# A piece of weight conversion four steps earlier in attention, and what follows it in the load queue

## The chip, the cores and the metric

The kernel runs on one core of a Trainium2 chip. The metric is the device time of one execution in microseconds. Engines: PE (matmul, with PEld for its weight loads), DVE (vector), ACT (scalar), POOL (GpSimd), and SP (SyncE), which issues nearly all DMAs here from one queue in program order.

## The reference

Three layers in fp32, one behind the other:

- attention with capped scores over 4 x 12 heads, 448 positions, 64 wide: `s = cap * tanh(q k^T / 8 / cap)`, softmax over the keys, times v. The result is read as x, 1792 tokens of 768.
- a soft mixture of 8 experts with 4 slots each: `logits = x @ phi`; a softmax over the tokens gives each slot its input `d^T x`; every expert computes `relu(slot @ w1[e]) @ w2[e]` (w1 768 x 1024, w2 1024 x 768); a softmax over the slots gives `c`, and the layer returns `c @ slot_out`.
- an MLP with a learnt slope: `h = x @ w_in`, `g = max(h, 0) + alpha * min(h, 0)`, `g @ w_out` (w_in 768 x 2048, w_out 2048 x 768).

`w_in`, `w_out` and `alpha` of the MLP come to the chip as the reference draws them; w_in and w_out arrive as 64-bit numbers (pairs of 32-bit words), which the kernel turns into fp32 itself.

## The kernel before, in words

**Attention** (lines 227 to 755) works on 24 pairs of heads. A pair has four steps, one for each chunk of keys, in the order CHUNKS = 0, 3, 1, 2 (chunk 3 is the short tail of the keys of both heads). Step `g` (line 702) issues `qk` of pair `g // 4` (scores on PE, then Tanh and Exp on ACT into a tile `p` of the pool `pt`), in the second step of a pair also the transposes of the next pair's k and q (`trans_k`, `trans_q`, with DVE and ACT passes for the high and low parts), then background work that was put off with `later` (row sums `rs`, norms `rb`, natural x `nx`, logits `lg`, `lr`, slot sums `ss`), then loads and conversions, and last `pv` of two steps before (matmuls `o`; POOL adds the rows of p into `acc`, lines 396, 400, 403). So p has its readers two steps after it is written. The program is handed to a scheduler that orders each engine's instructions; every engine then runs its own list in order.

**Conversion of w_in.** w_in is cut in 24 pieces of 128 x 512. A buffer `cvbuf` (line 652), which is one of the eleven 12 KB weight slots (number NA - 1 = 10), holds two raw pieces and two converted halves. `cv_at(n)` (line 663) names the step of piece n: 4, 6, 9, 13, 17, 21, ... and 93 for piece 23, the second step of pair 23. `conv_w_in` (line 667) is one ACT pass and four DVE passes (`to_f32`, lines 178 to 190). Two steps later `store_w_in` (line 673) writes the piece to a scratch tensor in HBM and loads the raw piece n + 2. After the last store the slot joins the free list.

**Weight loads.** `loads` (lines 81 to 89) is the order in which weights are fetched: w1 and w2 of the experts in halves of 12 KB per partition, then w_in and w_out. In attention `load_next` (line 121) may run in the fourth step of the pairs in LOADS (line 55), if a slot is free: ten of the eleven slots are filled at pairs 2 to 20, the entry 22 finds none free, and the entry 23 fills slot 10 behind the last store. `load_early` (line 116) fetches QE = 1 quarter (3 KB per partition) of the twelfth load in pair 21, into a tile of its own.

**Tail** (lines 757 to 1033). Behind attention's pools, which end there, a pool `xtra` takes their memory for seven more slots in quarters of 3 KB (line 1018): 27 loads (line 111, the twelfth load's first quarter is there already). Each of them waits for the attention tiles that it lies on. Then `experts` (line 800) runs expert by expert: h (line 810), ReLU, transposes, y (line 832). `done_with` frees a slot when its weight has been used, and `load_free` issues the next load into it, on SP's queue behind all earlier ones. After expert 7, `gather` and `mlp` (line 862): the first layer (`a_block`, line 870, and `hidden`), and the second (lines 941 to 948) with w_out split in high and low parts (`split_wo`).

**Attention's pools** lie behind the weight slots in the order of lines 232 to 246: nat0, nat1 (q and k as loaded, 4,096 bytes each), stk0 (transposed, 7,680), vn0 (1,792), acc0 (3,584), stk1 (7,680), pt (four buffers, 14,336 with the padding of the short chunk's), vn1, acc1, aconst0 (sel, hot, phi: 4,096), xn (7 x 1,792), xu (4 x 2,048), xnat (2 x 2,048), sm, aconst. Even pairs use the pools with 0, odd ones those with 1. The xtra quarters lie over them in steps of 3,072 bytes, quarter 0 at nat0's start.

Of the kernel before, what the change touches and what calls it, by code (L numbers as in the profile page):

```python
# [8 lines left out]
F32 = mybir.dt.float32  # L9
# [15 lines left out]
def tile_attention_soft_moe_mlp(ctx, tc, q, k, v, cap, phi, w1, w2, w_in, w_out, alpha, out):  # L25
    nc = tc.nc
    B, H, S, D = q.shape
    J = 4
# [4 lines left out]
    NSLOT = phi.shape[1]  # L33
# [12 lines left out]
    JK = 3  # L46
# [5 lines left out]
    LAG = 2  # L52

    CHUNKS = (0, 3, 1, 2)
    LOADS = (2, 4, 6, 8, 10, 12, 14, 16, 18, 20, 22, 23)

    EH = 5
    TBS = (4, 2, 2, 2, 2, 2)
# [38 lines left out]
    def may_load():  # L97
        if nload[0] == len(loads):
            return None
        late = loads[nload[0]][0] in ("wi", "wo")  # L100
        fit = [n for n in free if not late or n < NA]
        return fit[0] if len(fit) > (late and kept[0] < NWO) else None
# [124 lines left out]
    def attention():  # L227
        with ExitStack() as pools:
            def pool(name, bufs=1, **kw):
                return pools.enter_context(tc.tile_pool(name=name, bufs=bufs, **kw))  # L230
# [4 lines left out]
            v_0 = pool("vn0")  # L235
            acc_0 = pool("acc0")
            stk_1 = pool("stk1")
            pt_p = pool("pt", 4)
            v_1 = pool("vn1")
            acc_1 = pool("acc1")  # L240
            ac0_p = pool("aconst0")
# [3 lines left out]
            sm_p = pool("sm")  # L245
# [12 lines left out]
            phi_rep = ac_p.tile([128, 128], F32, name="phi_rep")  # L258
            z_run = ac_p.tile([128, 1], F32, name="z_run")

            def head(u):
                return slice(64 * u, 64 * u + 64)
# [6 lines left out]
            nat, stk, sc_t, pt, acc, ov, xu, xn = {}, {}, {}, {}, {}, {}, {}, {}  # L269
# [7 lines left out]
            def matmul(*a, **kw):  # L277
                ins = nc.tensor.matmul(*a, **kw)  # L278
                if order:
                    if order[0] is not None:  # L280
                        tc.add_manual_dep(ins.ins, order[0].ins.name, NOSYNC, reason="tilings together")
                    order[0] = ins
                return ins
# [81 lines left out]
            def qk(i, c):  # L365

                kh, kl = stk["k", i]
                qh, ql = stk["q", i]
                ps = ps_s.tile([128, 2, 512], F32, tag="s", name="s")
                for n, (a, b) in enumerate(((kh, qh), (kh, ql), (kl, qh))):  # L370
                    flags = dict(start=(n == 0), stop=(n == 2))
                    if c == JK:
                        matmul(ps[:, 0, :S], a[:, KEYS:], b, **flags)
                        continue
                    for u in range(2):
                        o = 128 * c
                        matmul(ps[:, u, :S], a[head(u), o:o + 128], b[head(u)], **flags)
                n = 1 if c == JK else 2
                pe = pt_p.tile([128, n, S], F32, tag="p", name="p")
                nc.scalar.activation(out=pe, in_=ps[:, :n, :S], func=AF.Tanh)  # L380
                nc.scalar.activation(out=pe, in_=pe, func=AF.Exp, scale=cap_sb)  # L381
                pt[i, c] = pe
# [277 lines left out]

            ncv = KD * (DFF // 512)

            def cv_at(n):

                return J + 2 * n if n < 2 else J * n + 1

            def conv_w_in(i):
                fb, kk = divmod(i, KD)
                t = cvbuf[:, 2, i % 2 * 512:i % 2 * 512 + 512].bitcast(F32)
                to_f32(craw.pop(i), t, (order[0], latest[0]))  # L670
                cout[i] = t
# [30 lines left out]
            for g in range(NPAIR * J + LAG):  # L702
                now[0] = g
                i, c = divmod(g, J)
# [4 lines left out]
                if i < NPAIR:  # L709
                    qk(i, CHUNKS[c])  # L710
                    if c == 1 and i + 1 < NPAIR:
                        trans_k(i + 1)
                        trans_q(i + 1)
                run_bg()
                if i < NPAIR:
                    if c == 0:
                        last = load(i + 2, "kq") or last
                    if c == 2:
                        if i == NPAIR - LAG - 1:
                            load_early(last)  # L720
                    if g == 2:
                        load_w_in(0)
                        load_w_in(1)
                    for n in range(ncv):
                        if cv_at(n) == g - 2:
                            store_w_in(n)
                        if cv_at(n) == g:
                            conv_w_in(n)
                    if c == 3 and i in LOADS and may_load() is not None:
                        load_next(last)  # L730
                if g >= LAG:
                    n, e = divmod(g - LAG, J)
# [7 lines left out]

            nc.vector.tensor_scalar(out=z_run, in0=z_run, scalar1=1e-9, scalar2=None, op0=ALU.add)
            nc.vector.reciprocal(out=z_run, in_=z_run)
            diag = sm_p.tile([128, NSLOT], F32, tag="diag", name="diag")
            nc.vector.tensor_scalar(
                out=diag, in0=stackI[:, 0:NSLOT], scalar1=z_run, scalar2=None, op0=ALU.mult
            )
# [10 lines left out]
    def tail():  # L757
# [254 lines left out]
        with (  # L1012
# [3 lines left out]
            with tc.tile_pool(name="ex2", bufs=1, reuse_waits="tile", side="right") as ex2_p:  # L1016
# [6 lines left out]
                with (  # L1023
# [9 lines left out]
                    mlp(ps_w, ps_c, ex_p, cv_p, g_p, ob_p, so, cstk)  # L1033

    attention()
    tail()

# [29 lines left out]
```

## Time and profile before

| | us |
|---|---|
| median of 3 runs | 623.11 (621.99 to 629.77) |
| the profiled execution | 622.67 |
| its span, first to last instruction | 620.7 |
| PE busy | 578.6 (93%) |
| DVE busy | 394.7 (64%) |
| ACT busy | 319.3 (51%) |
| POOL busy | 160.1 (26%) |
| DMA from HBM to the chip and back | 98.41 MB read, 11.80 MB written |

Attention ends at about 274 us, the experts at about 349, and the rest is the MLP. A busy share is an average over these three stages. Times in the rows are counted from the span's start. PE's matmuls are pipelined, so a row of x8 may overlap its neighbours by some tenths of a microsecond. "[2.65 <-DMA w<-...]" behind a row is the idle time of that engine before it and what ended it.

### The profile page before, as it was taken

What the parts mean: (1) busy time and instruction counts of PE and PEld (TensorE: products, weight loads), DVE (VectorE), ACT (ScalarE), POOL (GpSimd) and SP (SyncE); (2) the same over time, 40 slices, a digit from 0 to 9 for tenths busy, and PEclk for the clock granted to TensorE, in tenths of its full rate; (3) what the DMA queues carried; (4) which work ended last, traced back from release to release, by engine and by line L of the source; (5) the groups of instructions that cost most, each with busy time, mean ns of one, the idle gap of its engine ahead of it and who ended that gap; (6) DMA issues with size and microseconds to landing.
All of it is one profiled execution on the core that took longest, in us unless ns stands there. A gap on an engine that the chain in (4) does not pass through costs nothing.

```text
span 620.7 us, 10735 instructions
## 1 busy us (share of the span) xinstructions
PE 578.6 (93%) x4110; PEld 384.7 (62%) x4110; DVE 394.7 (64%) x734; ACT 319.3 (51%) x509; POOL 160.1 (26%) x111
## 2 busy tenths in 40 slices
PE   6799898999999999989896899999999999999996
PEld 4344344455445445454452568888888888888886
DVE  4568667696769879640013399999566666666662
ACT  4798898888889687420101266764412121121211
POOL 0668668475848457100000000000000000000000
PEclk9899999999999999979998899999999999999999
DMA  4786897887978661599999999200301001010101
GB/s 103 199 260 158 260 265 214 261 213 210 262 227 265 207 171 53 194 373 370 403 404 407 389 402 408 102 1 1 103 1 51 1 21 32 0 52 2 51 1 51
DMA packets 95169, 110.90 MB, mean 179 GB/s; under 512 B 56208, under 2 KB 70032, under 8 KB 95120
## 3 DMA queue, kind: packets, MB, share of 16 engines
q1 hardware_dynamic: 94976, 110.24, 55.0%
q8 instruction: 32, 0.52, 0.3%
q14 instruction: 17, 0.14, 0.1%
q10 hardware_dynamic: 144, 0.00, 0.0%
HBM read 98.41 MB, written 11.80 MB: 178 GB/s over the span
## 4 chain that ended last, share of the span: by engine, by line
PE 64%; DMA 15%; DVE 8%; ACT 7%; POOL 3%; issue 1%; SPq 1%; ACTq 0%; POOLq 0%
PE oc L941 13%; PE oc L947 13%; PE oc L948 13%; DMA w<-in_moe_w_dram 12%; PE o L278 6%; PE s L278 5%; ACT p L381 2%; PE hps L896 2%; PE aps L870 2%; ACT p L380 2%; DMA q<-in_q_dram 2%; POOL acc L400 2%; PE rs L278 1%; DMA cvbuf<-in_moe_w_in_dram 1%; PE nx L278 1%
## 5 line engine op out<-in xcount | busy, mean ns | idle before, releaser
L947 PE MATMUL oc<-wsp,gh 128*128 128x512 f32 x448 | 151.7, 339 | 0.0
L941 PE MATMUL oc<-wsp,gh 128*128 128x512 f32 x448 | 151.6, 338 | 0.0
L948 PE MATMUL oc<-wsp,gl 128*128 128x512 f32 x448 | 150.7, 337 | 0.0
L912 ACT ACTIVATE gh<-gf 128x256 fp32r<-128x256 f32 (+1 forms) x96 | 43.5, 453 | 133.0 <-DVE gf L911 127.1
L278 PE MATMUL o<-p,v 128*64 128x448 f32 (+1 forms) x384 | 94.0, 568 | 10.1 <-ACT xu L405 10.0
L380 ACT ACTIVATE p<-s 128x896 f32<-128x896 f32 x96 | 79.0, 824 | 28.6 <-PE s L278 19.7
L381 ACT ACTIVATE p<-p,cap 128x896 f32<-128x896 f32 x96 | 91.2, 951 | 2.3
L941 PEld LDWEIGHTS oc<-wsp,gh 128*128 128x128 f32 x448 | 85.0, 190 | 10.7 <-issue 0.9
L948 PEld LDWEIGHTS oc<-wsp,gl 128*128 128x128 f32 x448 | 84.7, 189 | 11.1 <-issue 1.2
L947 PEld LDWEIGHTS oc<-wsp,gh 128*128 128x128 f32 x448 | 85.0, 190 | 9.7 <-issue 0.4
L913 DVE TENSOR_TENSOR gl<-gf,gh 128x256 fp32r<-128x256 f32 (+1 forms) x96 | 45.0, 469 | 45.3 <-ACT gh L912 45.2
L396 POOL TENSOR_TENSOR acc<-p 128x896 f32<-128x896 f32 x24 | 53.0, 2207 | 77.8 <-ACT p L381 77.8
L278 PEld LDWEIGHTS s<-qh,kh 64*128 64x128 f32 (+1 forms) x168 | 18.1, 186 | 67.1 <-ACT p L380 26.1
L400 POOL TENSOR_TENSOR acc<-acc,p 64x448 f32<-64x448 f32 x46 | 54.3, 1180 | 3.1
L908 DVE TENSOR_SCALAR mn<-hps,alpha 128x256 f32<-128x256 f32 (+1 forms) x81 | 39.5, 487 | 23.6 <-PE hps L896 23.5
L403 POOL TENSOR_TENSOR acc<-acc,p 128x896 f32<-128x896 f32 x23 | 49.0, 2129 | 1.8
L278 PE MATMUL s<-qh,kh 64*128 64x448 f32 (+1 forms) x168 | 45.8, 475 | 0.0
L278 PEld LDWEIGHTS o<-p,v 128*64 128x64 f32 (+1 forms) x384 | 19.0, 134 | 34.8 <-ACT xu L405 16.4
L911 DVE SCALAR_TENSOR_TENSOR gf<-hps,mn 128x256 f32<-128x256 f32 (+1 forms) x81 | 34.6, 427 | 2.7
L278 PE MATMUL s<-qh,kl 64*128 64x448 f32 (+1 forms) x168 | 35.5, 367 | 0.0
L278 PE MATMUL s<-ql,kh 64*128 64x448 f32 (+1 forms) x168 | 35.3, 365 | 0.0
L810 PE MATMUL h<-w,slotT 128*32 128x256 f32 x384 | 30.6, 418 | 4.5 <-DMA w<-in_moe_w_dram 4.5
(151 smaller groups left out, 771.6 us busy)
## 6 DMA issues: line engine op xcount, KB each, us to landing
w<-in_moe_w_dram SPq DMA_DIRECT2D x80, 384.0 KB, 8.4
w<-in_moe_w_dram SPq DMA_DIRECT2D x36, 512.0 KB, 8.2
cvbuf<-in_moe_w_in_dram SPq DMA_DIRECT2D x24, 512.0 KB, 4.5
w<-in_moe_w_out_dram SPq DMA_DIRECT2D x16, 768.0 KB, 8.9
w_in<-cvbuf SPq DMA_DIRECT2D x24, 256.0 KB, 2.4
q<-in_q_dram SPq DMA_DIRECT2D x48, 112.0 KB, 4.0
k<-in_k_dram SPq DMA_DIRECT2D x48, 96.0 KB, 5.1
v<-in_v_dram SPq DMA_DIRECT2D x24, 192.0 KB, 3.4
```

What stands on the lines that cost most here:

```text
L278: ins = nc.tensor.matmul(*a, **kw)
L380: nc.scalar.activation(out=pe, in_=ps[:, :n, :S], func=AF.Tanh)
L381: nc.scalar.activation(out=pe, in_=pe, func=AF.Exp, scale=cap_sb)
L396: nc.gpsimd.tensor_add(out=a, in0=pt[i, 0], in1=pe)
L400: nc.gpsimd.tensor_add(out=a[r, u, :], in0=a[r, u, :], in1=pt[i, JK][r, 0, :])
L403: nc.gpsimd.tensor_add(out=a, in0=a, in1=pe)
L908: nc.vector.tensor_scalar(out=mn, in0=ps, scalar1=0.0, scalar2=alpha_sb[:, f:f + 1], op0=ALU.min, op1=ALU.mult)
L912: nc.scalar.activation(out=gh, in_=gf, func=AF.Copy)
L913: nc.vector.tensor_sub(out=gl, in0=gf, in1=gh)
L941: ins = nc.tensor.matmul(o, gh[:, ts], wo_h[f][:, cols], start=(f == 0 and not second), stop=False)
L947: nc.tensor.matmul(o, gh[:, ts], wo_l[f][:, cols], start=False, stop=False)
L948: nc.tensor.matmul(o, gl[:, ts], wo_h[f][:, cols], start=False, stop=(f == KF - 1 and not more))
```

## The change

The steps of the pieces come from a list: 4, 7, 10, 13, 16, 19, 22, 25, 29, and from there every fourth step, so that piece 23 is converted in step 89, the second of pair 22, and stored in step 91. LOADS has 21 and 22 for its last two entries. The pool `pt` has three buffers, and the short chunk's p has a pool of its own with one buffer of 1,792 bytes. `diag` takes the first columns of `phi_rep` and needs no tile.

```diff
-    LOADS = (2, 4, 6, 8, 10, 12, 14, 16, 18, 20, 22, 23)
+    LOADS = (2, 4, 6, 8, 10, 12, 14, 16, 18, 20, 21, 22)
...
-            pt_p = pool("pt", 4)
+            pt_p = pool("pt", 3)
+            ptt_p = pool("ptt")
...
-                pe = pt_p.tile([128, n, S], F32, tag="p", name="p")
+                pe = (ptt_p if c == JK else pt_p).tile([128, n, S], F32, tag="p", name="p")
...
+            cv_steps = [4, 7, 10, 13, 16, 19, 22, 25, 29]
+            while len(cv_steps) < ncv:
+                cv_steps.append(cv_steps[-1] + J)
+
             def cv_at(n):
-
-                return J + 2 * n if n < 2 else J * n + 1
+                return cv_steps[n]
...
-            diag = sm_p.tile([128, NSLOT], F32, tag="diag", name="diag")
+            diag = phi_rep[:, :NSLOT]
```

## Rows read from the trace of the kernel before

**Rows 1.** Windows, 360 to 370 us: PE, PEld, DVE, ACT, POOL busy, clock, DMA share, GB/s.

```profile
360.00:370.00 10.00, 10.00 (x57) 5.67 (x56) 9.68 (x16) 6.31 (x12) 0.00 (x0) 1.00 1.03 409
```

**Rows 2.** The chain of waits in order of time, 225 to 360 us: start, length, what.

```profile
340.73 7.88 DMA w<-in_moe_w_dram
348.65 0.63 PE y L832 x6
```

**Rows 3.** Windows around and after attention's end, columns as in rows 1.

```profile
246.40:254.50 8.10, 7.96 (x63) 3.40 (x63) 5.34 (x10) 6.85 (x9) 4.27 (x3) 1.00 0.10 34
...
264.00:284.00 20.00, 16.98 (x195) 10.60 (x197) 6.47 (x21) 3.00 (x8) 0.59 (x2) 0.83 1.07 371
284.00:324.00 40.00, 36.47 (x524) 19.94 (x520) 3.91 (x15) 3.51 (x13) 1.59 (x6) 1.00 1.04 395
324.00:350.00 26.00, 18.96 (x184) 7.06 (x177) 6.04 (x10) 2.50 (x4) 0.31 (x1) 0.87 1.04 399
```

**Rows 4.** DMA share in tenths, 40 slices of the span (15.5 us each).

```profile
DMA  4786897887978661599999999200301001010101
```

**Rows 5.** Timeline of SP's queue, 215 to 350 us: start, length, line, tiles, count.

```profile
244.32 6.93 SPq L675 DMA_DIRECT2D w_in<-cvbuf  x2
254.54 1.76 SPq L157 DMA_DIRECT2D w<-in_moe_w_dram  x4
256.34 28.26 SPq L111 DMA_DIRECT2D w<-in_moe_w_dram  x27
```

**Rows 6.** Issue to landing: the two stores of 244 to 251, then the 27 quarters.

```profile
DMA to landing us min/median/max: 2.0/2.7/3.5
...
DMA to landing us min/median/max: 6.5/8.6/9.4
```

**Rows 7.** Timeline of PE, the last two experts.

```profile
322.22 2.94 PE L810 MATMUL h<-w,slotT 128*32 128x256 f32 x47
...
328.33 2.51 PE L832 MATMUL y<-w,hT 128*32 128x256 f32 x30
...
334.45 0.64 PE L810 MATMUL h<-w,slotT 128*32 128x256 f32 x8 [2.65 <-DMA w<-in_moe_w_dram]
```

**Rows 8.** Timeline of PE, attention's end and expert 0.

```profile
253.37 0.55 PE L278 MATMUL rs<-acc,hot 128*32 128x224 f32 x6
...
256.64 1.07 PE L278 MATMUL rs<-p,hot 128*32 128x224 f32 x16
...
269.69 1.06 PE L278 MATMUL ss<-xu,dl 112*32 112x128 f32 x32
...
274.16 4.51 PE L810 MATMUL h<-w,slotT 128*32 128x256 f32 x48
```

**Rows 9.** The tile cvbuf: ns min/median/max of a pass; ACT's idle time before one.

```profile
L178 ACT ACTIVATE cvbuf<-cvbuf x24: 657/672/686, 21.7 to 247.1; 128x512 f32<-128x512 f32 x24
L179 DVE TENSOR_SCALAR cvbuf<-cvbuf x24: 408/417/1522, 22.3 to 247.9; 128x512 f32<-128x512 f32 x24
L183 DVE TENSOR_SCALAR cvbuf<-cvbuf x24: 417/427/2214, 23.9 to 249.0; 128x512 uint32<-128x512 uint32 x24
L186 DVE SCALAR_TENSOR_TENSOR cvbuf<-cvbuf x24: 681/693/1520, 24.8 to 249.5; 128x512 uint32<-128x512 uint32 x24
L189 DVE SCALAR_TENSOR_TENSOR cvbuf<-cvbuf x24: 680/692/2573, 26.0 to 250.2; 128x512 uint32<-128x512 uint32 x24
...
  DMA cvbuf<-in_moe_w_in_dram: 1.7, 1
```

**Rows 10.** Windows, pairs 3 to 5, columns as in rows 1.

```profile
43.00:62.50 19.50, 17.43 (x114) 8.05 (x110) 17.07 (x23) 17.39 (x24) 14.32 (x9) 1.00 0.75 190
```

**Rows 11.** Timelines of DVE and POOL at piece 22's last pass.

```profile
241.83 2.47 DVE L189 SCALAR_TENSOR_TENSOR cvbuf<-cvbuf 128x512 uint32<-128x512 uint32 x1
...
240.82 2.92 POOL L396 TENSOR_TENSOR acc<-p 128x896 f32<-128x896 f32 x1 [3.06 <-ACT p L381]
```

## The prediction, made before the changed kernel was run

> **What bounds the kernel now.** I read the profile from its end backwards. The last stage, the MLP, has no slack: PE is busy 10.00 of 10 us at full clock [rows 1], so whatever moves its start moves the end by as much. Before it the chain of waits is one unbroken run of weight transfers up to 348.61 us, and the last six matmuls of the last expert (y) start 0.04 us after the last one [rows 2]. So the expert stage ends with a DMA stream. The windows show that stream: from 264 us on, the 16 DMA engines are full (share 1.04 to 1.07, 371 to 399 GB/s), but from 246.40 to 254.50 they are almost idle (0.10, 34 GB/s) [rows 3]. The row of slices says the same: a 1 in the sixteenth slice (232.8 to 248.3 us), a 5 behind it, then nines [rows 4]. The stream is therefore late because it starts late.
>
> Why it starts late is on SyncE's queue [rows 5]. In attention's last pairs SyncE does little but wait: the store of w_in piece 22 goes at 244.32, that of piece 23 at 250.92 (244.32 + 6.93 - 0.33), and only behind that, at 254.54, come the four quarters for the slot that was the conversion buffer, and at 256.34 the 27 quarters that lie on attention's own memory. The gap from 250.92 to 254.54 is the last store landing (3.5 us, the longer of the two [rows 6]).
>
> The expert stage is not DMA-bound all along. PE works without a wait on DMA through the next-to-last expert (h from 322.22, y to about 331.2), and waits in the last: 2.65 us before its first h, then 0.2 to 0.6 us before almost every group [rows 7]. Seven experts were on chip or ahead; the eighth is late.
>
> **The change part by part.**
>
> *Last piece four steps earlier.* Pieces from the ninth on (index 8) move up one place: index 8 goes at step 29, where index 7 went, and index 23 at step 89, where index 22 went. Pair 23 has no conversion. So the store that now goes at 244.32 becomes the last one. It lands 2.0 us later (the shorter of the two [rows 6]; 3.5 is the other bound), and the slot's four quarters follow at about 254.54 - 250.92 - 3.5 = 0.1 us behind the landing: 244.32 + 2.0 + 0.1 = 246.4, against 254.54. The stream starts 8.1 us earlier (6.6 with a landing of 3.5). The step's queue order allows it: the store frees the slot and the load stands right behind it in the same step (LOADS has 22); the last v load on SyncE is two steps before. LOADS' 21 finds no free slot and does nothing.
>
> *Do the next quarters follow?* They wait in order for attention's buffers. By the shapes in the code, quarters 0 to 4 lie on q and k of pairs 22 and 23 as loaded and on pair 22's transposed ones, all read by step 91, the step of the store at 244.32; 5 and 6 on the sums of pair 22, read by rs until 253.92; 10 to 14 on pair 23's p and acc, read until 257.71; 15 to 19 on sel, phi and xn, read before ss starts at 269.69; 20 to 24 on xu and xnat, which ss reads until 270.75 [rows 8]. The 27 issues took 28.26 us, 1.05 each [rows 5], so quarter k would now be due at 248.2 + 1.05 k: the fifth at 253.5, the tenth at 258.7, the twentieth at 269.2 (with the pools behind pt 1,792 bytes lower it is number 20, no longer 21, that first touches xu), the load behind them at 276.6. That last one needs the slots of expert 0's h, which ends at 274.16 + 4.51 = 278.67 [rows 8]. So issues wait 0.4, 0, 1.6 and 2.1 us (number 15, due at 264.0, 5.7 at the very most), each below the 8.6 us that a transfer spends in flight behind others [rows 6]: the engines don't run dry, and the stream keeps its lead.
>
> *What the lead is worth.* 8.1 us if each transfer takes as long as before; if the extra stretch runs at the 371 GB/s of 264 to 284 and saves time at 399 [rows 3], 8.1 x 371/399 = 7.5. I take 7.9, nearer to the first, because a lead of the whole queue carries each transfer's own length with it. Its cover on the other side: the last y ends at 348.65 + 0.63 = 349.3, so 341.4 then; PE alone, from 331.2 with the 9.0 us of the expert before it (322.22 to 331.2), would reach 340.2 [rows 7]. So DMA still ends last, by about 1 us, and more than 9.1 us can't be had here.
>
> The Trainium skill, DMA: Bandwidth & Descriptors (Where 436 GB/s comes from), says that HBM to SBUF is held to about 358 GB/s for a core. The trace disagrees: 395 and 399 GB/s over 66 us [rows 3]. By that rule the lead would give 8.1 x 358/399 = 7.3.
>
> *First nine three steps apart.* Steps 6, 9, 17, 21 and 93 become 7, 10, 16, 19 and 22. The work is the same: each conversion has one ACT pass of 0.672 us and four DVE passes of 0.417 + 0.427 + 0.693 + 0.692 = 2.23 us [rows 9]. One more of them falls into the first 25 steps, one fewer into the last pair. Load (512 KB) and store of a piece move with it; the pieces get four steps or more from load to conversion, as most have now; the one wait of ACT on such a landing in the whole run, 1.7 us [rows 9], is the first piece's, and that stays at step 4. In two of the cases (steps 11 and 19) store and load of w_in no longer stand just before a slot's load, and the q and k behind them can only gain. DVE from 43.0 to 62.5 is busy 17.07 of 19.50 and ACT 17.39 [rows 10]; one more conversion takes DVE to 19.3, just inside. If the passes of ACT at steps 9, 17 and 21 come off the path the gain is 3 x 0.672 = 2.0 us, if all five new places cost theirs the loss is 3.4; I take 0 and keep both.
>
> *Pools and diag.* pt held four buffers in a cycle of four, chunk by chunk the same; three and a separate one give every chunk the same distance to its former reader: 0. Both bounds are 0 because no wait changes. diag in phi_rep's place overwrites a tile whose last reader, the last logits matmul, stands before the softmax that diag waits for anyway: 0. The 1,920 bytes freed are under the 3,072 that one more early quarter takes, and the diff leaves QE at 1: I find no extra early quarter. With one, 1.0 us more would be saved (393,216 bytes at 395 GB/s).
>
> **Sum.** The profiled execution took 622.67 us (span 620.7 and 2.0 around it): 622.67 - 7.9 = 614.8. The median of the runs shown is 0.44 above that execution, so I forecast 615.
>
> **The rivals.**
>
> *The queue starves behind attention's buffers.* Only the slot's four quarters come early, then SyncE stands until the old time because a later quarter waits for more than I read from the shapes. For it: SyncE is in order, and a quarter touches up to three tiles. Against: 5 is the first one with a late reader. Four quarters at 1.0 us each: 4.0 saved, 618.7.
>
> *Attention gets longer (slower).* The moved conversions fall beside POOL's adds. The row shows what that does: the last pass of piece 22 took 2.47 us instead of 0.69 while POOL's add ran from 240.82 to 243.74 [rows 11], and the four maxima add to 1.522 + 2.214 + 1.520 + 2.573 = 7.83 against 2.23, 5.6 more [rows 9]. Five of them lose 28.0 at most; DVE's slack of 2.43 in 19.5 us [rows 10] gives 5.4 over the 16 steps concerned (98 steps end at about 266 us, 2.7 each: 43 us); 22.6 remain, less 7.9: 14.7 slower, 637. The sign turns where the five lose 13.3 together, 2.7 each. Against: the maxima are single passes, and the medians say that most passes meet no add.
> The Trainium skill, SBUF — State Buffer (SBUF: two separate sides), says why: VectorE passes in a two-port mode or with two SBUF inputs and GpSimd's share one pair of ports, and the one that starts second waits for the whole of the other. By that rule every moved conversion can meet it; the 2.47 us pass, ending 0.56 after the add's end, agrees.
>
> *Attention gets shorter as well.* The 2.0 us of ACT above come off and q lands earlier: 612.8 or a little under. For it: the queue is shorter at steps 11 and 19. Against: POOL and PE are nearly full too.
>
> *It doesn't do what it says.* The slot is not free in pair 22 and loads at the old time: 622.7. Against: the store appends the slot before the load asks.
>
> **How the numbers follow.** Forecast (613 to 617) 0.60; starved queue 0.17; shorter attention 0.10; no effect 0.05; slower 0.08. The range takes in the starved queue, the gain of 2.0 with an extra quarter, and the loss of 3.4 with a landing of 3.5: 611 to 621, about 0.83. 2% is 12.5 us, about what a measurement of this kernel can tell from no change: faster needs under 610.7, beyond what PE leaves in the expert stage, 0.05; slower needs over 635.6, the disturbed conversions nearly at their maximum, 0.03; within 2%: 0.92.
>
> **What would show it.** After the change: SyncE's row of the slot's quarters at about 246.4; DMA share near 1 from 248 us on; h of expert 0 still at 274; the last y at about 341, its waits on DMA shorter; MLP unchanged in length. Wrong if the share falls below 0.9 for more than 2 us between 250 and 285, if expert 0 starts later than 276, or if the last expert waits for PE's own work and the end moves by less.

## The result: 0.9% faster, with a last store 8 us earlier within attention and an attention that is 4 us longer

| | before | after |
|---|---|---|
| median of 20 runs each | 624.25 us | 618.36 us |
| ratio, 95% interval | | 0.9909 [0.9885, 0.9934], about -5.7 us |
| profiled execution, its span | 622.67, 620.7 | 618.59, 616.2 |
| last score tile of attention (step 95) starts | 252.33 | 256.12 |
| last store of w_in issued, landed | 250.93, 254.38 | 248.12, 250.12 |
| the slot's quarters issued | 254.54 | 250.26 |
| last y of the expert stage ends | 349.29 | 345.01 |

The forecast was 615; the median came 3.4 us above it, outside the narrow range of 613 to 617 and inside the wide one of 611 to 621. Each ratio here and below is taken against runs of before made beside that kernel's (median 624.25 here, 622.86 to 623.42 for the experiments), and two single runs far above the rest (712.54 us of e5, 798.61 of before) are left out of it. The table says where the 3.4 went. In the profiled execution the slot's quarters left 4.3 us earlier and not 8.1, because the end of attention runs 3.8 us late. First SP's queue after the change (start, length, line, tiles, count), which answers to [rows 5]:

```profile
248.12 0.33 SPq L680 DMA_DIRECT2D w_in<-cvbuf  x1
250.26 1.76 SPq L157 DMA_DIRECT2D w<-in_moe_w_dram  x4
252.07 29.08 SPq L111 DMA_DIRECT2D w<-in_moe_w_dram  x27
```

The store lands 2.0 us later, the quarters follow 0.14 behind, and the 27 go at 1.08 us each (forecast 1.05): as forecast, only 3.9 us later than forecast. (In the changed kernel the lines of the helpers are one higher and those behind the conversions five.) ScalarE's row of the last score tile, before and then after, has the same 3.8:

```profile
252.33 0.92 ACT L380 ACTIVATE p<-s 128x896 f32<-128x896 f32 x1
```

```profile
256.12 0.92 ACT L381 ACTIVATE p<-s 128x896 f32<-128x896 f32 x1
```

The windows of after (columns as in rows 1), to set beside [rows 1, 3], and its slices of DMA share beside [rows 4]:

```profile
246.40:250.30 3.90, 3.56 (x30) 1.82 (x27) 3.27 (x5) 2.94 (x5) 3.76 (x3) 1.00 0.18 67
250.30:264.00 13.70, 13.46 (x107) 5.69 (x107) 7.34 (x13) 7.30 (x10) 4.21 (x2) 1.00 0.93 318
264.00:284.00 20.00, 17.18 (x144) 10.96 (x144) 8.05 (x24) 3.71 (x9) 0.00 (x0) 0.74 1.07 370
284.00:324.00 40.00, 36.25 (x508) 21.18 (x511) 3.48 (x15) 3.68 (x14) 1.56 (x5) 1.00 1.03 401
324.00:345.00 21.00, 18.78 (x249) 9.52 (x248) 6.16 (x10) 2.41 (x4) 0.62 (x2) 1.00 1.03 399
355.50:365.50 10.00, 10.00 (x56) 5.63 (x55) 9.68 (x16) 6.31 (x12) 0.00 (x0) 1.00 1.02 408
```

```profile
DMA  4778877798887781799999999100301010010101
```

From 250 us on the stream is nearly full (share 0.93 up to 264, 1.02 or more behind it), and the MLP has no slack, as before. In the row of slices the trough is one slice (1, then 7) instead of a 1 and a 5. PE's timeline (answers to [rows 7, 8]) shows the changed end of the expert stage:

```profile
273.98 1.93 PE L279 MATMUL ss<-xu,dl 112*32 112x128 f32 x32
...
279.42 4.29 PE L815 MATMUL h<-w,slotT 128*32 128x256 f32 x48
...
335.74 2.94 PE L815 MATMUL h<-w,slotT 128*32 128x256 f32 x47
...
343.38 0.63 PE L837 MATMUL y<-w,hT 128*32 128x256 f32 x6 [0.36 <-DMA w<-in_moe_w_dram]
344.38 0.63 PE L837 MATMUL y<-w,hT 128*32 128x256 f32 x6 [0.37 <-DMA w<-in_moe_w_dram]
```

The last expert's h no longer waits for DMA (2.65 us before its first group in [rows 7]); only the last groups of y do, by 0.4. PE and the stream now end within a microsecond of each other.

**The account of the profiled execution.** Between the start of step 95's tile and the slot's quarters lay +2.21 us, now -5.86: the place of the last piece brings 8.07 (the store 6.60 earlier, its landing 2.00 instead of 3.45). Attention gives back 3.79. From the slot's quarters to the last y it is 94.75 us in both. The rest of the span is 0.18 shorter, what lies around the span 0.38 longer. -8.07 + 3.79 - 0.18 + 0.38 = -4.08, the difference of 618.59 and 622.67. The medians differ by 5.9, since this execution of before lies 1.6 below its median and that of after 0.2 above its own; the ratio gives 5.7.

### The profile page after: what moved, and what is told of

Its sections match the earlier page's. It is cut to its first block, busy times and chain, and to the rows that moved or that the text cites. A ratio compares the mean times of both kernels' runs of the same rounds, so it can differ in the third digit from the quotient of the medians.

```text
span 616.2 us, 10737 instructions
## 1 busy us (share of the span) xinstructions
PE 574.9 (93%) x4110; PEld 386.6 (63%) x4110; DVE 403.6 (65%) x734; ACT 318.8 (52%) x509; POOL 162.4 (26%) x111
## 4 chain that ended last, share of the span: by engine, by line
PE 64%; DVE 11%; DMA 10%; ACT 7%; POOL 4%; issue 2%; SPq 1%; ACTq 0%; POOLq 0%
PE oc L946 13%; PE oc L952 13%; PE oc L953 13%; DMA w<-in_moe_w_dram 7%; PE o L279 5%; PE s L279 5%; PE hps L901 2%; ACT p L382 2%; POOL acc L401 2%; PE aps L875 2%; POOL acc L397 2%; ACT p L381 2%; DMA k<-in_k_dram 2%; PE h L815 2%; PE tr L279 1%
## 5 line engine op out<-in xcount | busy, mean ns | idle before, releaser
L837 PE MATMUL y<-w,hT 128*32 128x256 f32 x384 | 30.7, 382 | 1.8 <-DVE hT L830 1.1
```

## Why attention is longer, read from the two traces

Four microseconds do not come at once. Against before, the score tile of step 13 starts 0.7 later, that of step 21 0.6, of step 22 2.8, of step 37 4.05, and from step 42 on every tile is 3.8 late. The largest step, 2.2 us, is that from 21 to 22, behind the second conversion of pair 4. The other 1.6 (0.6 up to step 21 and 1.0 from step 22 to 42) was not traced. GpSimd's timeline of before in this stretch (in brackets the idle time ahead):

```profile
55.41 2.35 POOL L396 TENSOR_TENSOR acc<-p 128x896 f32<-128x896 f32 x1 [2.35 <-ACT p L381]
57.83 2.67 POOL L400 TENSOR_TENSOR acc<-acc,p 64x448 f32<-64x448 f32 x2
60.57 2.11 POOL L403 TENSOR_TENSOR acc<-acc,p 128x896 f32<-128x896 f32 x1
65.07 2.10 POOL L396 TENSOR_TENSOR acc<-p 128x896 f32<-128x896 f32 x1 [2.39 <-ACT p L381]
```

Per pair GpSimd adds without a break for 7 us and has one gap, of 2.4 us. The conversion in VectorE's timeline of before stands exactly in the gap from 62.68 to 65.07:

```profile
62.79 0.42 DVE L179 TENSOR_SCALAR cvbuf<-cvbuf 128x512 f32<-128x512 f32 x1
63.25 0.43 DVE L183 TENSOR_SCALAR cvbuf<-cvbuf 128x512 uint32<-128x512 uint32 x1
63.71 0.69 DVE L186 SCALAR_TENSOR_TENSOR cvbuf<-cvbuf 128x512 uint32<-128x512 uint32 x1
64.43 0.69 DVE L189 SCALAR_TENSOR_TENSOR cvbuf<-cvbuf 128x512 uint32<-128x512 uint32 x1
```

62.79 to 65.12: 2.33 us in a gap of 2.39. The second conversion of pair 4 after the change has no gap. GpSimd, then VectorE, of after:

```profile
56.05 2.45 POOL L397 TENSOR_TENSOR acc<-p 128x896 f32<-128x896 f32 x1 [2.27 <-ACT p L382]
58.57 2.50 POOL L401 TENSOR_TENSOR acc<-acc,p 64x448 f32<-64x448 f32 x2
61.15 2.43 POOL L404 TENSOR_TENSOR acc<-acc,p 128x896 f32<-128x896 f32 x1
67.83 2.11 POOL L397 TENSOR_TENSOR acc<-p 128x896 f32<-128x896 f32 x1 [4.26 <-ACT p L382]
```

```profile
57.99 0.79 DVE L179 TENSOR_SCALAR cvbuf<-cvbuf 128x512 f32<-128x512 f32 x1
58.81 1.25 DVE L183 TENSOR_SCALAR cvbuf<-cvbuf 128x512 uint32<-128x512 uint32 x1
60.09 1.52 DVE L186 SCALAR_TENSOR_TENSOR cvbuf<-cvbuf 128x512 uint32<-128x512 uint32 x1
61.65 2.48 DVE L189 SCALAR_TENSOR_TENSOR cvbuf<-cvbuf 128x512 uint32<-128x512 uint32 x1
64.05 0.61 DVE L487 TENSOR_TENSOR xn<-xu,rb 128x448 f32<-128x448 f32 x1
```

Each pass ends just behind one add (0.3 to 0.55 us): one pass per add, 6.14 us instead of 2.33 (57.99 to 64.13). Attention's own xn stands behind them on VectorE, xu on ScalarE waits 2.06 for xn, and o on PE 2.25 for xu:

```profile
64.75 0.55 ACT L406 ACTIVATE xu<-o 128x448 f32<-128x448 f32 x1 [2.06 <-DVE xn L487]
```

```profile
65.35 0.97 PE L279 MATMUL o<-p,v 128*64 128x448 f32 x4 [2.25 <-ACT xu L406]
```

ScalarE's next score tile, that of step 22, stands behind xu and starts at 65.76. GpSimd's next pair then starts late: 4.26 idle instead of 2.39. The Trainium skill, SBUF — State Buffer (SBUF: two separate sides), agrees: an operation of VectorE in a two-port mode or with two SBUF inputs and one of GpSimd exclude each other for a whole instruction.

## The experiments

What each run's profile shows, one execution each, in us from its span's start ("second conversion" names the step of the one that shares a pair with another, beyond those of before):

| kernel | last conversion | second conversion | tile of step 95, against before | slot's quarters | last y ends | quarters to last y |
|---|---|---|---|---|---|---|
| before | 93 | | 0 | 254.54 | 349.29 | 94.75 |
| before again | 93 | | +1.3 | 255.73 | 350.12 | 94.4 |
| after | 89 | 19 | +3.8 | 250.26 | 345.01 | 94.75 |
| e1, steps alone | 89 | 19 | +4.2 | 250.70 | 345.00 | 94.3 |
| e2 | 93 | 19 | +4.1 | 256.81 | 351.61 | 94.8 |
| e3 | 89 | 58 | +9.3 | 255.83 | 349.94 | 94.1 |
| e4, fewer passes | 89 | 19 | -0.2 | 246.27 | 340.91 | 94.6 |
| e5 | 91 | 91 | +8.7 | 255.63 | 350.48 | 94.9 |
| e6 | 89 | 83 | +4.1 | 248.46 | 344.24 | 95.8 |
| e7 | 89 | 11 | +4.8 | 251.29 | 345.80 | 94.5 |
| e9 | 89 | 19 | +2.3 | 248.75 | 343.60 | 94.9 |
| e10 | 93 | | +1.2 | 255.72 | 350.79 | 95.1 |
| e11 | 92 | | +3.9 | 258.17 | 352.47 | 94.3 |
| e12, fewer passes | 89 | 19 | +7.6 | 254.15 | 349.09 | 94.9 |

Two things can be read at once. The last column moves by 1.7 at most (94.1 to 95.8) while the start moves by 12: nearly all that the stream's start gains or loses reaches the end of the expert stage. And the start is attention's length plus the place of the last piece.

**Which part of the change does it.** The kernel before with the new list of steps alone:

```diff
-                return J + 2 * n if n < 2 else J * n + 1
+                return cv_steps[n]   # [4, 7, 10, 13, 16, 19, 22, 25, 29, 33, ...]
```

> The kernel before with the new list of conversion steps alone; pools, diag and LOADS as before. If the steps are the whole change: a span of 616.2 us within 0.5, the slot's quarters issued at 250.3, score tiles of step 95 about 3.8 us later than before. If the pools, diag or LOADS have a part: a span nearer to 620.7 or a different shift in attention.

618.32 us (one run); attention 4.2 longer, last y at 345.00. The first expectation came out: the steps are the whole change, and the pools, diag and the list of load steps move nothing that can be seen in one execution.

**The two effects apart.** The new early places, the last piece back at 93:

```diff
+            cv_steps[-1] = 93
-    LOADS = (2, 4, 6, 8, 10, 12, 14, 16, 18, 20, 21, 22)
+    LOADS = (2, 4, 6, 8, 10, 12, 14, 16, 18, 20, 22, 23)
```

> The changed kernel with the first nine pieces three steps apart, but the last piece back in step 93 (LOADS 22, 23). If the three-step spacing costs attention 3.8 us by itself: step 95 about 3.8 us later than before, the slot's quarters at about 254.5 + 3.8 = 258.3, and an end 3 to 4 us later than before, 626 to 627 (ratio about 1.006). If the attention is longer for another reason, such as the last piece's place or the pools: as before, 622.7.

625.06 us, ratio 1.0024 [0.9996, 1.0052]. Attention is 4.1 longer; the last store goes 3.4 later, but lands after 2.3 us instead of 3.45, so that the quarters leave 2.3 later and not 3.8. So the early places by themselves bring nothing; that they cost something is seen in the profile, while by the times no change is not excluded. Against this kernel, after differs in the place of the last piece (and the two load steps) alone: its quarters leave 6.55 earlier, its last y ends 6.60 earlier, and its ratio is 0.9909 instead of 1.0024. This is the lead, without a change of the early places.

**The vector passes taken out.** In the kernel after, pieces 1, 2, 4, 5 and 6 keep only ScalarE's pass:

```diff
-                to_f32(craw.pop(i), t, (order[0], latest[0]))
+                if i in (1, 2, 4, 5, 6):
+                    ins = nc.scalar.activation(
+                        out=t, in_=craw.pop(i)[..., 1].bitcast(F32), func=AF.Abs, scale=65536.0
+                    )
+                    tc.add_manual_dep(ins.ins, order[0].ins.name, NOSYNC, reason="not before its step")
+                else:
+                    to_f32(craw.pop(i), t, (order[0], latest[0]))
```

> The changed kernel without the four vector passes of the five moved pieces (1, 2, 4, 5, 6): their scalar pass, their store and their loads stay, and what is stored for them is the scalar pass's result. If the vector passes beside POOL's adds are what lengthens attention: the shift of +3.8 us at step 40 goes to 0 or below (down to -2), the end to 614.5 or less. If the scalar pass in another place or the order of SyncE's queue is the cause: the shift stays at 3 to 4 us and the end at 617 to 618.

613.91 us (one run, 3.0 below the fastest of 20 of after). SP's queue, and PE's last y:

```profile
244.12 0.33 SPq L686 DMA_DIRECT2D w_in<-cvbuf  x1
246.27 1.76 SPq L157 DMA_DIRECT2D w<-in_moe_w_dram  x4
```

```profile
340.27 0.63 PE L843 MATMUL y<-w,hT 128*32 128x256 f32 x6 [0.35 <-DMA w<-in_moe_w_dram]
```

The forecast had 244.32, 246.4 and 341.4 for these three. With the passes gone everything else of the prediction comes out: attention is as long as before's (0.2 shorter), and the stream's term is confirmed. So what attention pays for is in the passes. The run takes out twenty of them, though, and doesn't only put them elsewhere.

**Another place for the one conversion more.** The twenty-four conversions stood in 23 pairs, one in each and two in the first of them. If the last pair has none, another must have two. Old early places, the extra one in pair 14:

```diff
+            cv_steps = [4, 6, *range(9, 54, J), 56, 58, *range(61, 90, J)]
```

> The changed kernel with the pieces at their old steps and the additional conversion in pairs 14 to 15 (steps 56 and 58 instead of 57), where PE is busy for almost the whole pair. If the early crowding is what was lost and DMA ends the expert stage: attention as before within 1 us, the slot's quarters at 246.4 to 247.4, the last y at about 341 to 342, 614.7 to 616 (ratio about 0.987). If PE already bounds the expert stage, or an added conversion costs its 2 to 4 us in any pair: 617.5 to 618.5, as the changed kernel.

620.41 us, ratio 0.9956 [0.9914, 0.9999]. The passes of the extra conversion, in VectorE's timeline of this run:

```profile
159.81 2.10 DVE L179 TENSOR_SCALAR cvbuf<-cvbuf 128x512 f32<-128x512 f32 x1
161.94 1.24 DVE L183 TENSOR_SCALAR cvbuf<-cvbuf 128x512 uint32<-128x512 uint32 x1
163.22 1.51 DVE L186 SCALAR_TENSOR_TENSOR cvbuf<-cvbuf 128x512 uint32<-128x512 uint32 x1
164.77 2.44 DVE L189 SCALAR_TENSOR_TENSOR cvbuf<-cvbuf 128x512 uint32<-128x512 uint32 x1
```

7.4 us; attention is 4.9 longer behind it. (The other 4.4 arose before step 40, see below.) That the extra conversion is hidden in this pair fell; the times fit neither expectation, with five runs from 617.8 to 619.1 and five from 621.8 to 625.7. Three more places:

```diff
+            cv_steps = [4, 6, *range(9, 90, J), 91]                        # e5, LOADS ending 22, 23
+            cv_steps = [4, 6, *range(9, 78, J), 81, 83, 85, 89]            # e6
+            cv_steps = [4, 6, 9, 11, *range(13, 90, J)]                    # e7
```

> The kernel after with the old spacing of the early conversions (4, 6, 9, 13, ... every four) and only the last one moved, from step 93 to 91, behind the one at 89; the list of load steps ends in 22, 23 as before. Theory (the early places cost attention 3.8 us, the place of the last store sets the start of the stream): attention is as before up to step 89; the last store goes two steps earlier than before, at about 247.7, and lands by 249.7 to 251.2; the slot's quarters follow it, 3.4 to 4.8 us before the 254.54 of before; one more conversion in pair 22 (VectorE 12.2 of 12.9 us busy there) gives some of it back, up to 2.5. Last y at 345 to 348, 618 to 621 us. Rival (any moved or added conversion costs attention about what it saves, wherever it stands): last y at 349 or later, 622.5 or more.

> The kernel after with the old early places and the extra conversion in pair 20, where PE and not VectorE is the fullest engine (VectorE 7.5 of 11.5 us): places 4, 6, 9, 13, ... 77, 81, 83, 85, 89. Theory (a conversion costs attention where its passes stand beside GpSimd's adds and VectorE is needed next; in a pair that PE bounds it is hidden): attention within 1 us of before, the last store at about 244.5, the slot's quarters at 246.5 to 247.5, last y at 341 to 342, 614 to 615.5 us. Rival (an added conversion costs 4 to 5 us in any pair, as in pair 14): the slot's quarters at 251, last y at 346, 619 us.

> The kernel after with the old places and one extra conversion at step 11, in pair 2, where VectorE is least busy (4.7 of 9.1 us): places 4, 6, 9, 11, 13, 17, ... 85, 89; from the fourth piece on every piece is one place earlier. Theory: the passes of step 11 meet GpSimd's adds or not by where these stand in that pair; hidden by VectorE's 4.4 us if they miss, at most 4 us longer if they meet: the slot's quarters between 246.5 and 250.5, last y 341 to 345, 614 to 618.5 us. Rival (any added conversion costs 4 to 5): 619 us.

e5: 623.88, 0.9986 [0.9951, 1.0021]. e6: 618.48, 0.9941 [0.991, 0.9973]. e7: 619.13, 0.9941 [0.9919, 0.9964]. The first theory of e5 fell (attention grew by 5.8 at that place, and not by up to 2.5), and its rival's time came out. In e6 the step of the extra conversion cost nothing until step 85 and then 4.4 together, so the theory fell there too, with a last y between the two expectations. In e7 the rival's 619 came out. In all eight kernels of the next table the passes of the second conversion take 4.7 to 7.4 us from the first one's start to the last one's end, instead of 2.33, and attention grows:

| second conversion | its passes | attention longer by |
|---|---|---|
| e9, step 19 | 57.62 to 63.38 | 2.3 |
| after, step 19 | 57.99 to 64.13 | 3.8 |
| e2, step 19 | 59.66 to 64.34 (the pair's first one: 51.70 to 58.19) | 4.1 |
| e1, step 19 | 58.05 to 64.31 | 4.2 |
| e6, step 83 | 221.58 to 227.35 | 4.4 |
| e7, step 11 | 39.22 to 45.47 | 4.8 |
| e3, step 58 | 159.81 to 167.21 | 4.9 |
| e5, step 91 | 247.85 to 253.44 | 5.8 |

(Growth in the whole of attention for after, e1, e2, e7 and e9, around the step for the others. Between the passes stand other VectorE operations of 1.9 us in e6 and 0.7 in e5.) The length of the passes alone is not the price. The conversion of step 29, alone in its pair, took 2.33 us in before and stands beside the adds in e3, e5, e10 and e11; here its first and last pass in e11, 5.8 us together with the two between:

```profile
87.52 0.41 DVE L179 TENSOR_SCALAR cvbuf<-cvbuf 128x512 f32<-128x512 f32 x1
...
91.79 1.51 DVE L189 SCALAR_TENSOR_TENSOR cvbuf<-cvbuf 128x512 uint32<-128x512 uint32 x1
```

From step 25 to step 42 attention of these four runs moves by at most 0.4 us against before and by 1.3 against e6. Why a second conversion costs more than this one is not shown.

In e6 a part of it is PE's clock. PE stands idle for 3.34 us until VectorE has made the low part of k (1.03 in before); the windows (columns as in rows 1) of PE's idle time and of what follows:

```profile
226.00:229.00 3.00, 0.18 (x2) 0.22 (x3) 2.93 (x6) 1.22 (x3) 0.01 (x1) 0.93 0.41 136
229.00:236.00 7.00, 7.00 (x28) 2.91 (x27) 4.47 (x13) 2.70 (x4) 1.32 (x1) 0.54 0.45 144
```

After 0.18 us of work in 3 the granted clock is 0.54, near the lower of its two levels (1.2 of 2.4 GHz), and PE is busy for the whole of the next 7 us.

**Which of the new early places costs.**

```diff
+            cv_steps = [4, 6, 9, 13, 16, 19, 22, *range(25, 90, J)]        # e9
+            cv_steps = [4, 7, 10, *range(13, 94, J)]                       # e10, LOADS ending 22, 23
```

> The kernel after with the old places 4, 6, 9, 13 and then 16, 19, 22, 25, 29: pieces 1 and 2 stand where they stood, the one conversion more is the second one of pair 4. Theory A (a pair that holds two conversions pays about 4 us for the second, and the other moved places are free): the score tiles are 3.5 to 4.5 us later than before by step 37, the last y at 344.5 to 345.5, 618 to 619 us like the kernel after. Theory B (each moved place costs its share, five of them 3.8): about 2.3 us by step 37, last y 343.5, 617 us.

> The kernel after with only the moves 6 to 7 and 9 to 10: places 4, 7, 10, 13, 17, 21, ... 89, 93, no pair with one conversion more, list of load steps ending in 22, 23. Theory A: attention within 1.3 us of before, last store at 250.5 to 252.5, last y at 349 to 350.5, 622 to 623.5 us. Theory B: attention 1.5 us longer, 624. If place 10 avoids GpSimd's add that place 9 meets in some executions (the second piece's passes took to 42.4 instead of 37.4 us in two of the profiles), fewer of its runs than of before's lie above 625.

e9: 616.94 (5 runs), ratio 0.9899 [0.9863, 0.9935]. e10: 622.67, 1.0005 [0.9982, 1.0028]. By the times, moving pieces 1 and 2 costs nothing that can be seen, and the moves from piece 4 on alone bring what the whole change brings; by the profiles they cost 2.3 where after pays 3.8, which is theory B's number, but not its mechanism, a share from each place: 2.2 of the 2.3 come between the score tiles of steps 21 and 22, as in after and e1 (2.2 each). In e2, where the pair's first conversion ran long, 2.3 come between steps 19 and 20; in e4, without the passes, 0.0 come at step 22. So the second conversion of pair 4 cost 2.2 in three executions, and that it carries all 3.8 is not shown. In e10's profile attention is 1.2 longer, no more than in before again; place 10 did not avoid GpSimd's adds (piece 2's passes took 4.9 us), and one of its ten runs lies above 625, of before's 20 beside them four, too few to tell. The finer question was for e12, the kernel after without the vector passes of piece 5:

```diff
+                if i == 5:   # else as in the run without the passes of five pieces
```

> The kernel after; piece 5, the second conversion of pair 4 (step 19), keeps only its ScalarE pass, so that one of w_in's 24 stored pieces is not the converted values. Theory A (the second conversion of pair 4 is the 3.8 us): score tiles within 1.3 us of before from step 37 on, the slot's quarters at 246.3 to 247.6, last y at 341 to 342.3, 614 to 615.5 us. Theory B (five moved places share it): 2.5 to 3.2 us remain, last y at 343.7 to 344.4, 617 us.

622.24 us (one run), attention 7.6 longer with less work: neither theory. Piece 2's passes ran from 36.50 to 44.05 in this execution, and piece 3's from 46.06 to 53.28; most of the loss (7.1) was there by step 21. Between steps 21 and 22 only 0.4 came on top, where after, e1 and e9 lose 2.2. That points at piece 5, but with everything ahead of it in another place the run doesn't decide it.

**How far attention varies by itself.** The kernel before once more, and a kernel that came out as nearly that:

```diff
+            cv_steps = [4, 6, *range(9, 90, J), 92]                        # e11, LOADS ending 22, 23
```

> The kernel before, unchanged, profiled a second time, to see how far its own attention varies from one execution to the next. If the extra 3.8 us of attention in the kernel after belong to the new places, the score tiles of this run start within 1 us of the first profile's from step 13 to 95, and the last y ends at 349 to 350. If they belong to how GpSimd and VectorE happen to meet in an execution, the tiles of this run stand 2 us or more off the first profile's somewhere before step 40.

> The kernel after with the old places and the last conversion at step 92 instead of 93, the first step of the last pair: places 4, 6, 9, 13, ... 85, 89, 92, load steps ending in 22, 23. If the last pair hides a conversion wherever it stands in it (as at 93, where taking it away gained attention nothing): last store 2.5 to 3.5 us earlier than before, at 247.5 to 248.5, slot's quarters at 249.5 to 251.5, last y at 344.5 to 347, 617.5 to 620 us. If an early place in pair 23 costs what the one at 91 cost (5.8 us): last y at 349 to 351, 622.5 to 624 us.

Before again: 623.47 (one run), attention 1.0 to 1.3 longer from step 8 on, between the two expectations. e11: 622.16, 1.0005 [0.9971, 1.0039]; its expectation missed, and for a plain reason: the last conversion stands between the same two score tiles on ScalarE as with 93, so that its ScalarE and VectorE do attention in the order of before. Yet the profiled execution is 3.9 us longer in attention. VectorE and GpSimd of this run, at piece 2 of step 9:

```profile
36.57 0.41 DVE L179 TENSOR_SCALAR cvbuf<-cvbuf 128x512 f32<-128x512 f32 x1
37.01 2.21 DVE L183 TENSOR_SCALAR cvbuf<-cvbuf 128x512 uint32<-128x512 uint32 x1
39.26 1.51 DVE L186 SCALAR_TENSOR_TENSOR cvbuf<-cvbuf 128x512 uint32<-128x512 uint32 x1
40.80 1.52 DVE L189 SCALAR_TENSOR_TENSOR cvbuf<-cvbuf 128x512 uint32<-128x512 uint32 x1
```

```profile
36.82 2.11 POOL L397 TENSOR_TENSOR acc<-p 128x896 f32<-128x896 f32 x1 [2.52 <-ACT p L382]
39.02 2.75 POOL L401 TENSOR_TENSOR acc<-acc,p 64x448 f32<-64x448 f32 x2
```

and in before:

```profile
35.04 0.42 DVE L179 TENSOR_SCALAR cvbuf<-cvbuf 128x512 f32<-128x512 f32 x1
...
36.68 0.69 DVE L189 SCALAR_TENSOR_TENSOR cvbuf<-cvbuf 128x512 uint32<-128x512 uint32 x1
```

```profile
37.21 2.13 POOL L396 TENSOR_TENSOR acc<-p 128x896 f32<-128x896 f32 x1 [2.23 <-ACT p L381]
```

In before the passes are through by 37.38, all but the last 0.17 us in the gap; here they begin 1.5 us later, 0.25 ahead of the add, and end at 42.32. The store behind them on SP and the loads behind the store are late with them. The same is seen in e3 and e5 (piece 2 through at 42.3 and 42.4). One load of k stands earlier on SP's queue in e11 than in before, but that is not the cause, since e6 has it too: e3, e5, e6 and e11 have the same order of work on every engine and on SP's queue up to 120 us, and at step 42 attention stands at +4.4, +2.9, -0.2 and +3.9 against before. So executions with one order of work differ by up to 4.6 us, more than the 3.8 of after. It fits that the runs of these kernels fall into two groups some 4 us apart (e11: six from 620.8 to 622.3, four from 625.9 to 627.1): the profiles of e3, e5 and e11 are from the upper group, that of e6 is from the lower one.

## Why the prediction was right, and which step failed

- **Bounds and direction: right.** The stream was late because it started late, and its start was the last store's landing. Landing (2.0), the quarters 0.1 behind it, 1.08 us a quarter against 1.05, the MLP's constant length (271.4 and 271.2 us from the last y on): all nearly as worked out. "What the lead is worth" took 7.9 of 8.1; quarters to last y is 94.75 in both, so the lead is worth all of itself. One reading was a little off: the next-to-last expert's last y waits 0.32 for DMA and ends at 331.79, not 331.2, so PE's side left some 0.5 us less room than was worked out. It was enough.
- **The number of the rival "The queue starves", 618.7, is nearer to the result than the forecast, but its mechanism is not what happened.** The 27 quarters stand right behind the slot's four (252.07). Two of the waits that the prediction priced were longer: 2.9 for rs (0.4 forecast) and 3.1 for ss (1.6). The share fell to 0.76 for 2 us, and the stream kept its lead.
- **Pools, diag, LOADS: right,** as far as the one run with the steps alone shows. No further weight quarter came in attention.
- **"First nine three steps apart ... I take 0 and keep both": the term that was mis-sized.** It measured +3.8 in the profiled execution, above its bound of +3.4; by the ratio about 8.1 - 5.7 = 2.4. Of the 3.8, 2.2 come at step 22, in after, e1 and e9 alike; the rest is less than executions of one order differ by, and its cause stays open. The bound was five ScalarE passes of 0.672; the price is in VectorE's passes, as the one run without them shows. [Rows 10] were read as slack of VectorE, 2.43 us in 19.5, "just inside". In pair 4 it wasn't idle time that mattered but where it lies: GpSimd's adds leave one gap of 2.4 us per pair, which a conversion of 2.33 fills, and the second conversion stood beside the adds, with attention's xn behind it. The wide range held because its upper end carried a loss of 3.4 together with a landing of 3.5, and only the first of these was exceeded.
- **The rival "Attention gets longer" named the mechanism** and its row [rows 11] but asked when five conversions would lose 13.3 together. The question was one second conversion in a pair: attention longer by 2.3 to 5.8 us in eight profiles, which also hold what executions differ by.
- **"Expert 0 still at 274", "wrong if later than 276": failed without effect.** It starts at 279.42: 3.8 from attention, and the clock of 264 to 284 is 0.74 instead of 0.83 [rows 3] (ss took 1.93, 1.06 before). The stream and not PE ends the stage, and quarters to last y did not grow, so this cost nothing.
- **DMA share never below 0.9 for more than 2 us: at the limit.** It holds 0.93 from 250.3 to 264; inside that, 254.3 to 256.3 has 0.76, and up to 252 the late stream had only begun.

The best version is the kernel after or e9, 0.9909 and 0.9899 of before; their intervals do not tell them apart. e4 (613.91, without twenty passes) shows about how much the passes of the moved pieces still cost; how much of that another place could save is not shown.

## What to carry to other kernels

Before a step is moved into an engine's idle time, ask what the other user of the shared resource does in that time. Here VectorE's idle share said that there was room, and in pair 4 what counted was the time that GpSimd's adds leave free and the work of attention that waits behind the passes. When less than one per cent is at stake, read a second profile of the unchanged kernel before a difference of its early part is given a cause: executions with one order of work differed by 4.6 us here.

## What the runs showed of the hardware that was not expected

- Short VectorE passes beside a row of GpSimd adds go one per add: four that take 2.33 us alone took 6.14 in after and 7.41 in e3, with only a part of a microsecond lost on GpSimd's side in after (2.10 to 2.45 and 2.11 to 2.43 us an add).
- With the same order of work on ScalarE and VectorE up to that place, passes that arrived 1.5 us later went with 3.9 us more at step 18 (e11 against before), and 3.9 were still there 77 steps later.
- PE, kept idle for 3 us by VectorE in e6, then ran at a granted clock of 0.54 for 7 us.
